# First tile's centring, transposes and evacuation in halves, x ahead of the weight rows on ScalarE's queue, TensorE warmed on constants, variances by ScalarE

## Chip, cores, metric

One core of one Trainium2 chip. The metric is the device time of one execution in microseconds (us); three executions of the kernel before gave a median of 1615.57 us (1615.40 to 1615.64). All times inside a profile are counted from the start of its span.

## The reference, cut to what matters

Two layers, each a sliding-window attention block and a gated feed-forward block on x of 2048 tokens by 1024 columns. What matters here is the very beginning: layer norm of the first tokens, then their projection on the first 1024 columns of `wqkv`.

```python
def _layernorm(x, axis=-1, eps=1e-5):
    m = jnp.mean(x, axis=axis, keepdims=True)
    v = jnp.var(x, axis=axis, keepdims=True)
    return (x - m) / jnp.sqrt(v + eps)
...
    x = A_x                                              # (1, 2048, 1024), bf16
    x = x + _A_ref(_layernorm(x, axis=-1), A_wqkv, A_wo) # qkv = x @ wqkv; attention; @ wo
    x = x + _B_ref(_layernorm(x, axis=-1), B_w1, B_w3, B_w2)
    ...                                                  # the same two blocks once more
```

## The kernel before: the parts that count

The kernel records every operation in a small program (`pr.add`). A scheduler in Python (`place`) then gives each a modelled start time, from durations and a model of the transfers, and the operations are emitted in the order of those times. So the order on each engine follows from modelled times, and an edit can move operations that it does not touch.

The first stage works on four tiles of 128 tokens. Tiles 0 and 1 are only centred; their scale is applied later. They are transposed by TensorE, copied out of PSUM and projected against the eight weight rows (a "row" is 128 of the 1024 input columns, 256 KB) as these arrive. Tiles 2 and 3 are fully normalized, transposed and projected in a second half, which needs all eight rows.

```python
def q_first():
    for hh in range(2):                                  # x tile 0 in two halves, one on each queue
        dma(128, x_sb[0][:, hh * 512:(hh + 1) * 512], ..., queue="AQ" if hh else "SP")
    load_x(0, 1, 2)                                      # x tile 1, SyncE's queue
    rows = q_weights(0, "k", load=False)
    for kk in range(3):
        rows[2](kk, "SP" if kk == 1 else "AQ")           # rows 0 and 2 on ScalarE's queue
    load_x(0, 2, 4)                                      # x tiles 2 and 3
    for kk in range(3, KT):
        rows[2](kk)                                      # rows 3 to 7
    ...
    for j in range(2):
        dve(0.5, lambda _, j=j: nc.vector.tensor_scalar(xn[j][:], x_sb[j][:], mean[:, j:j + 1], None,
                                                        op0=ALU.subtract), ...)
        transposed(xn[j], ...)                           # 8 transposes, then two copies out of one bank
    for j in range(2, TPC):
        stats(j); root(j, j + 1); apply(j); transposed(xn[j], ...)
    for j in range(2):
        stats(j, [("xn", TPC - 1)]); root(j, j + 1); apply(j); dma(..., transpose=True)
    ...
    # projection of tiles 0 and 1: rows 0, 1, 2 by tile (8 matmuls each), rows 3 to 7 for both (8 wide ones each)
    for kk, j0, j1 in [(k, j, j + 1) for j in range(2) for k in range(3)] + [(k, 0, 2) for k in range(3, KT)]:
        ...
```

"AQ" is ScalarE's queue, "SP" SyncE's. Transfers share eight semaphores in turn, so a transfer's issue may first wait for the landing of the one that had its semaphore before.

Of the kernel before, what the change touches and what calls it, by code (L numbers as in the profile page):

```python
# [33 lines left out]
class Program:  # L34
# [28 lines left out]
    def place(self, n_banks=8, rate=330e3):  # L63
# [18 lines left out]
        banks = [0.0] * n_banks  # L82
        pipe = 0.0
        left = len(self.ops)
# [9 lines left out]
        while left:  # L94
# [28 lines left out]
            if e in ("SP", "AQ"):  # L123
                free[e] = t + op.dur
                begin = max(pipe, t + 1.3)
                pipe = begin + op.size / rate
                op.end = pipe + 0.8
            else:
                free[e] = t + op.dur
                op.end = t + op.dur + op.lag  # L130
# [24 lines left out]
def kernel(  # L155
# [42 lines left out]
    def alloc(name, shape, dt=BF16):  # L198
        return sb.tile(shape, dt, name=name)
# [4 lines left out]
    preload = alloc("preload", [P, 1], FP32)  # L204
    warm = alloc("warm", [P, CH])
    x_sb = [alloc(f"x{n}", [P, D]) for n in range(S // P)]
# [40 lines left out]
    def dve(dur, emit, reads, writes, cls=2, **kw):  # L247
        return pr.add("DVE", dur, emit, reads, writes, cls, **kw)
# [29 lines left out]
    pr.add("POOL", 0.1, lambda _: nc.gpsimd.memset(epst[:], EPS), writes=["eps"])  # L278
    dve(0.3, lambda _: nc.vector.memset(warm[:], 0.0), [], ["warm"], 0)
    act(1.5, lambda _: nc.scalar.activation(preload[:], epst[:], ACTF.Sqrt), ["eps"], ["preload"])  # L280
    for i in range(NWARM):
        a = Acc()
        pr.add("PE", 0.43, lambda op: nc.tensor.matmul(bank[op.takes[0].bank][:], lhsT=warm[:, 0:P], rhs=warm[:],
                                                       start=True, stop=True), reads=["warm"], takes=[a])

# [16 lines left out]
    def ln(c, first=False):  # L302
        s = stage_no[0]
        b, q = s % 2, s % 4
        xb = xnT[b]

        def stats(j, after=()):
            n = c * TPC + j
            pri = -9 if first else 1
            for hh in range(2):  # L310
                dve(0.67, lambda _, hh=hh: nc.vector.bn_stats(st[q][:, j, hh, :],  # L311
                                                              x_sb[n][:, hh * 512:(hh + 1) * 512]),
                    [("x", n, hh)] + list(after), [("st", q, j, hh)], pri)
            dve(0.2, lambda _: nc.vector.bn_aggr(mv[q][:, j, :], st[q][:, j, :, :]),  # L314
                [("st", q, j, 0), ("st", q, j, 1)], [("mv", q, j)], pri)

        def root(j0, j1):
            act(0.3, lambda _: nc.scalar.activation(sd[q][:, j0:j1], mv[q][:, j0:j1, 1], ACTF.Sqrt, bias=epst[:]),  # L318
                [("mv", q, j) for j in range(j0, j1)] + ["eps"], [("sd", q, j) for j in range(j0, j1)], -9 if first else 0, table="sqrt")
            dve(0.16, lambda _: nc.vector.reciprocal(rstd[q][:, j0:j1], sd[q][:, j0:j1]),  # L320
                [("sd", q, j) for j in range(j0, j1)], [("rstd", q, j) for j in range(j0, j1)], -9 if first else 0)

        def apply(j):
            n = c * TPC + j
            dve(0.5, lambda _: nc.vector.tensor_scalar(xn[j][:], x_sb[n][:], mv[q][:, j, 0:1], rstd[q][:, j:j + 1],  # L325
                                                       op0=ALU.subtract, op1=ALU.mult),
                [("x", n, 0), ("x", n, 1), ("mv", q, j), ("rstd", q, j)], [("xn", j)], -9 if first else 1)

        if first:
            return b, q, stats, root, apply  # L330
        for j in range(TPC):
            stats(j)
        root(0, TPC)
        for j in range(TPC):
            apply(j)
            dma(256, xb[:, :, j * P:(j + 1) * P], xn[j][:], [("xn", j)], [("xnT", b, j)], 0, transpose=True)
        return b
# [17 lines left out]
    def q_weights(which, split, load=True, after=()):  # L355
        ids = [take_slot(), take_slot()]
        if not load:
            def row(kk, queue="SP"):
                i = ids[kk // 4]
                v = slot[i][:].rearrange("p (k c) -> p k c", k=4)  # L360
                dma(256, v[:, kk % 4, :], wqkv_v[:, kk, which * D:(which + 1) * D], [], [("w", i, kk % 4)], 0,
                    queue=queue)
            return ids, split, row
# [28 lines left out]
    def q_tile(l, c, which, ws, b, keep=None):  # L392
        for m0 in range(0, KT, 2):
            i = n_sgt[0] % 4
            n_sgt[0] += 1
            for m in (m0, m0 + 1):
                a = Acc()
                lk = [q_lhs(ws, kk, m) for kk in range(KT)]
                op = mm8(a, [(w, xnT[b][:, kk, :]) for kk, (w, _) in enumerate(lk)], True, True,
                         list({k for _, k in lk}) + [("xnT", b, j) for j in range(TPC)])  # L400
                evac(act, 0.59, lambda _, a=a, i=i, m=m: nc.scalar.copy(sgt[i][:, m % 2, :], bank[a.bank][:]), op, [],  # L401
# [13 lines left out]

    def transposed(src, key, dst, dkeys, both):
        a = Acc()

        def tr(op):
            pt = bank[a.bank][:].bitcast(BF16)  # L420
            for kk in range(KT):
                nc.tensor.transpose(pt[:, kk * P:(kk + 1) * P], src[:, kk * P:(kk + 1) * P], ident[:])  # L422
        tro = pr.add("PE", 0.5, tr, [key, "ident"], [], takes=[a], lag=0.17, lane=2)

        def ev(add, fn, k0, k1, dur):
            def emit(op):
                pt = bank[a.bank][:].bitcast(BF16)
                fn(dst[:, k0:k1, :], pt.rearrange("p (k t) -> p k t", k=KT)[:, k0:k1, :])
            evac(add, dur, emit, tro, [], dkeys[k0:k1], a, cls=-9)
        if both:  # L430
            ev(dve, nc.vector.tensor_copy, 0, 4, 0.68)
            ev(act, nc.scalar.copy, 4, 8, 0.59)
        else:
            ev(act, nc.scalar.copy, 0, 8, 1.0)

    def q_first():
        for hh in range(2):
            dma(128, x_sb[0][:, hh * 512:(hh + 1) * 512], xin[:, 0, hh * 512:(hh + 1) * 512], [], [("x", 0, hh)], 0,
                queue="AQ" if hh else "SP")
        load_x(0, 1, 2)  # L440
        rows = q_weights(0, "k", load=False)
        wslots[0] = rows[:2]
        for kk in range(3):
            rows[2](kk, "SP" if kk == 1 else "AQ")
        load_x(0, 2, 4)
        for kk in range(3, KT):
            rows[2](kk)
        b, q, stats, root, apply = ln(0, first=True)
# [4 lines left out]
        act(0.75, lambda _: nc.scalar.activation(xn[3][:, 0:512], x_sb[0][:, 512:1024], ACTF.Copy,  # L453
                                                 accum_out=part[:, 1:2]), [("x", 0, 1)], [("xn", 3), ("part", 1)], -9)
        dve(0.16, lambda _: nc.vector.tensor_scalar(mean[:, 0:1], part[:, 0:1], part[:, 1:2], 1.0 / D, op0=ALU.add,
                                                    op1=ALU.mult), [("part", 0), ("part", 1)], [("mean", 0)], -9)
# [3 lines left out]
        for j in range(2):  # L460
            dve(0.5, lambda _, j=j: nc.vector.tensor_scalar(xn[j][:], x_sb[j][:], mean[:, j:j + 1], None,  # L461
                                                            op0=ALU.subtract),
                [("x", j, 0), ("x", j, 1), ("mean", j)], [("xn", j)], -9)
            transposed(xn[j], ("xn", j), ce[:, :, j * P:(j + 1) * P], [("ce", j, k) for k in range(KT)], True)
        for j in range(2, TPC):
            stats(j)
            root(j, j + 1)
            apply(j)
            transposed(xn[j], ("xn", j), xnT[b][:, :, j * P:(j + 1) * P], [("xnT", b, j)] * KT, False)
        for j in range(2):  # L470
            stats(j, [("xn", TPC - 1)])
            root(j, j + 1)
            apply(j)
            dma(256, xnT[b][:, :, j * P:(j + 1) * P], xn[j][:], [("xn", j)], [("xnT", b, j)], 0, transpose=True)
# [27 lines left out]
        for g in range(4):  # L502
            lk = [[q_lhs(wslots[0], kk, m)[0] for kk in range(KT)] for m in (2 * g, 2 * g + 1)]

            def emit(op, g=g, lk=lk, pa=pa):
                for m in range(2):
                    for kk in range(KT):
# [3 lines left out]
            ops.append(pr.add("PE", 16 * 0.1092, emit,  # L511
                              [("w", i, k) for i in wslots[0][0] for k in range(4)] + [("xnT", b, 2), ("xnT", b, 3)],
                              [], takes=[pa[g]], lag=0.17))
# [10 lines left out]
        for which, key, tile_ in ((1, "kT", kT), (2, "vT", vT)):  # L524
            dve(0.11, lambda _, tile_=tile_: nc.vector.memset(tile_[:, :, 0:HALO], 0.0), [], [(key, "h")], 1)
            q_tile(0, 0, which, wslots[which], b, (key, tile_))
        for t0, t1_ in ((0, 2), (2, 4), (4, 6), (6, 7), (7, 8)):
            dma(256 * (t1_ - t0), wo[:, t0:t1_, :], wo_v[:, t0:t1_, :], [("d", 0, 2, 0, 6)], [("wo", t0)], 3)
# [26 lines left out]
    def t_stage(l, half):  # L555
# [54 lines left out]
        for j in range(TCH // P):  # L610
            n = tok0 // P + j
            for hh in range(2):
                a = Acc()
                op = mm8(a, [(oT[oh][:, t, j * P:(j + 1) * P], wo[:, t, hh * 512:(hh + 1) * 512]) for t in range(KT)],
                         True, True, [("oT", oh, t) for t in range(KT)] + [("wo", t) for t in (0, 2, 4, 6, 7)], lane=1)
                xs = x_sb[n][:, hh * 512:(hh + 1) * 512]
# [5 lines left out]
    def b_stage(l, c):  # L622
        b = ln(c)
        allx = [("xnT", b, j) for j in range(TPC)]
        for g0 in range(0, NF, 4):
# [119 lines left out]
```

## Time and profile before

| | before |
|---|---|
| median of 3, us | 1615.57 |
| TensorE busy | 100% |
| TensorE's last pause ends | 6.89 us |
| first projection matmul | 7.34 us |
| first of the 64 second-half matmuls | 15.28 us |
| first K matmul (first 512-wide one on data) | 22.27 us |
| first K matmul's start to last matmul's start | 1588.615 us |

The last three numbers come from the trace's list of matmul starts. They make a precise instrument: the body from the first K matmul to the last matmul never pauses, so its time is fixed, and whatever the first stage gains or loses is read off the start of the first K matmul.

Next, from the page of the kernel before, are the shares of the chain of waits: first by engine, then by line. In all lines of the profile PE is TensorE, PEld its weight loads, DVE VectorE, ACT ScalarE, SP SyncE; a q behind it (ACTq) marks what the engine's sequencer does itself, such as issuing a transfer.

```profile
PE 99%; DMA 0%; ACT 0%; DVE 0%; SPq 0%; issue 0%; ACTq 0%
PE bank L344 98%; PE bank L494 0%; PE bank L508 0%; DMA x<-in_A_x_dram 0%; PE bank L422 0%; ACT xn L457 0%; DVE xn L461 0%; SPq L260 0%; DVE x L672 0%; ACTq L457 0%
```

TensorE is the whole chain. Only its start can move. The timeline of TensorE in the kernel before, from 3 to 16 us, has the start in us, the time covered, engine, line, operation, tiles, shape, count, and in brackets the idle time before it and what ended it:

```profile
5.25 0.62 PE L422 MATMUL bank<-ident,xn 128*128 128x128 bf16 x8 [0.28 <-DVE xn L461]
6.89 0.62 PE L422 MATMUL bank<-ident,xn 128*128 128x128 bf16 x8 [1.02 <-DVE xn L461]
7.34 5.46 PE L494 MATMUL bank<-hT,slot 128*128 128x128 bf16 x72
12.64 1.06 PE L422 MATMUL bank<-ident,xn 128*128 128x128 bf16 x16
13.54 1.91 PE L494 MATMUL bank<-hT,slot 128*128 128x256 bf16 x16
15.28 0.93 PE L508 MATMUL bank<-xnT,slot 128*128 128x256 bf16 x7
```

L422 are the transposes, L494 the projection of tiles 0 and 1, L508 that of tiles 2 and 3. The pause of 1.02 us is a wait for tile 1's centring. Tile 0 has been transposed since 5.87 us but stands behind tile 1 everywhere: its projection in TensorE's order, and the first half of its copy out of PSUM in VectorE's, after tile 1's centring (ScalarE began the second half at 6.22, after tile 1's sum):

```profile
6.34 0.49 DVE L461 TENSOR_SCALAR xn<-x,mean 128x1024 bf16<-128x1024 bf16 x1 [1.15 <-ACT xn L457]
6.81 0.42 DVE L428 COPY hT<-bank 128x512 bf16<-128x512 bf16 x1
```

(Matmuls overlap, so idle time as the view has it is some 0.16 us less than the distance between starts in excess of full pace.)

### The profile page before, as it was taken

The numbers are of one execution on the slowest core, as the hardware profiler recorded it, in microseconds if no ns is written. First come the engines' busy times: TensorE is split into PE (matmuls) and PEld (weight loads), VectorE is DVE, ScalarE is ACT, GpSimd is POOL, SyncE is SP. The second block draws the span as 40 slices with busy tenths as digits, with TensorE's granted clock in tenths as the row PEclk, the third lists the DMA queues.
The fourth block names the chain that finished last, engine by engine and source line by source line (L and its number), as shares of the span: only waits on it lengthen the run. The fifth ranks groups of instructions, "written<-read, shape, count | busy, mean of one in ns | idle before, by whom it ended". The sixth has DMA issues, their size and how long they took to land.

```text
span 1613.7 us, 19216 instructions
## 1 busy us (share of the span) xinstructions
PE 1608.6 (100%) x7610; PEld 762.6 (47%) x7610; DVE 1123.6 (70%) x1908; ACT 326.8 (20%) x521; POOL 4.9 (0%) x28
## 2 busy tenths in 40 slices
PE   9999999999999999999999999999999999999999
PEld 6555544444444444444444444444444444444444
DVE  5898888989888888988888829884288832211211
ACT  4423322021201222113211032110321101101110
POOL 1000000000000000000000000000000000000000
PEclk9999999999999999999999999999999999999999
DMA  9834755485548764858554487355873564454441
GB/s 313 234 103 151 221 170 171 131 211 170 171 137 250 195 190 133 216 167 243 181 161 134 160 243 231 123 171 176 251 225 118 157 183 156 144 174 152 156 164 45
DMA packets 350651, 285.80 MB, mean 177 GB/s; under 512 B 72290, under 2 KB 344930, under 8 KB 350562
## 3 DMA queue, kind: packets, MB, share of 16 engines
q1 hardware_dynamic: 350128, 283.94, 58.6%
q8 instruction: 59, 0.97, 0.3%
q10 hardware_dynamic: 432, 0.66, 0.1%
q14 instruction: 32, 0.25, 0.1%
HBM read 238.94 MB, written 29.36 MB: 166 GB/s over the span
## 4 chain that ended last, share of the span: by engine, by line
PE 99%; DMA 0%; ACT 0%; DVE 0%; SPq 0%; issue 0%; ACTq 0%
PE bank L344 98%; PE bank L494 0%; PE bank L508 0%; DMA x<-in_A_x_dram 0%; PE bank L422 0%; ACT xn L457 0%; DVE xn L461 0%; SPq L260 0%; DVE x L672 0%; ACTq L457 0%
## 5 line engine op out<-in xcount | busy, mean ns | idle before, releaser
L344 PE MATMUL bank<-xnT,slot 128*128 128x512 bf16 x5056 | 1094.2, 379 | 0.0
L344 PEld LDWEIGHTS <-slot 128*128 128x128 bf16 x5056 | 518.1, 102 | 573.0
L344 PE MATMUL bank<-slot,hT 128*128 128x512 bf16 (+2 forms) x1848 | 389.2, 373 | 0.0
L642 DVE TENSOR_TENSOR hT<-sg,bank 128x512 bf16<-128x512 bf16 x224 | 153.4, 685 | 215.7 <-PE bank L344 203.4
L264 DVE TENSOR_TENSOR scr<-scr 128x1024 bf16<-128x1024 bf16 (+3 forms) x576 | 292.9, 539 | 2.0
L344 PEld LDWEIGHTS <-hT 128*128 128x128 bf16 x1848 | 178.6, 98 | 208.7
L640 ACT ACTIVATE sg<-bank 128x512 bf16<-128x512 f32 x224 | 133.7, 597 | 662.6 <-PE bank L344 625.3
L264 DVE TENSOR_TENSOR scr<-qT,kT 128x2048 bf16<-128x2048 bf16 x128 | 154.1, 1220 | 72.1 <-DMA kT<-qkv_d 70.7
L401 ACT CAST sgt<-bank 128x512 bf16<-128x512 f32 x184 | 107.5, 586 | 349.7 <-PE bank L344 345.5
L264 DVE TENSOR_TENSOR scr<-pA,vT 128x2048 bf16<-128x2048 bf16 x128 | 152.3, 1220 | 0.3
L672 DVE TENSOR_TENSOR x<-x,bank 128x512 bf16<-128x512 bf16 (+1 forms) x66 | 43.9, 670 | 123.4 <-PE bank L344 123.4
L344 PE MATMUL bank<-wo,oT 128*128 128x512 bf16 x512 | 113.1, 379 | 0.0
L311 DVE BATCH_NORM_STATS2 st<-x 128x6 f32<-128x512 bf16 x128 | 84.3, 680 | 10.6 <-DMA x<-in_A_x_dram 10.2
L344 PEld LDWEIGHTS <-oT 128*128 128x128 bf16 x512 | 50.1, 98 | 60.3
L617 DVE TENSOR_TENSOR x<-x,bank 128x512 bf16<-128x512 bf16 x64 | 43.9, 685 | 31.5 <-PE bank L344 30.6
L600 DVE STREAM_TRANSPOSE pA<-pB 128x2048 bf16<-128x2048 bf16 x16 | 37.0, 2311 | 0.5
L577 DVE STREAM_TRANSPOSE pB<-pA 128x2048 bf16<-128x2048 bf16 x16 | 37.0, 2310 | 0.4
L264 DVE TENSOR_TENSOR pA<-scr 128x256 bf16<-128x256 bf16 x128 | 35.8, 286 | 0.4
L318 ACT ACTIVATE sd<-mv,epst 128x4 f32<-128x4 f32 (+1 forms) x19 | 5.7, 299 | 143.8 <-DVE mv L314 143.7
L325 DVE TENSOR_SCALAR xn<-x,mv,rstd 128x1024 bf16<-128x1024 bf16 x64 | 32.0, 541 | 3.5 <-DMA xnT<-xn 3.3
L640 ACT ACT_TABLE_LOAD x19 | 24.4, 1283 | 49.4 <-PE bank L344 49.2
L264 DVE TENSOR_TENSOR oT<-scr 128x256 bf16<-128x256 bf16 x128 | 33.9, 288 | 0.1
(55 smaller groups left out, 203.8 us busy)
## 6 DMA issues: line engine op xcount, KB each, us to landing
slot<-in_B_w_dram SPq DMA_DIRECT2D x160, 1024.0 KB, 5.9
slot<-in_A_wqkv_dram SPq DMA_DIRECT2D x28, 1024.0 KB, 5.2
qkv_d<-sgt SPq DMA_DIRECT2D x92, 256.0 KB, 3.5
qT<-qkv_d SPq DMA_DIRECT2D x16, 512.0 KB, 4.8
slot<-in_B_w_dram SPq DMA_DIRECT2D x16, 512.0 KB, 5.8
kT<-qkv_d SPq DMA_DIRECT2D x14, 544.0 KB, 5.9
vT<-qkv_d SPq DMA_DIRECT2D x14, 544.0 KB, 5.9
out_dram<-x SPq DMA_DIRECT2D x31, 128.0 KB, 4.4
```

Of the source, the lines that this page charges most:

```text
L264: return lambda _: nc.vector.tensor_tensor(o, a, b, op=op)
L311: dve(0.67, lambda _, hh=hh: nc.vector.bn_stats(st[q][:, j, hh, :], x_sb[n][:, hh * 512:(hh + 1) * 512]), [("x", n, hh)] + list(after), [( ...
L318: act(0.3, lambda _: nc.scalar.activation(sd[q][:, j0:j1], mv[q][:, j0:j1, 1], ACTF.Sqrt, bias=epst[:]), [("mv", q, j) for j in range(j0, ...
L325: dve(0.5, lambda _: nc.vector.tensor_scalar(xn[j][:], x_sb[n][:], mv[q][:, j, 0:1], rstd[q][:, j:j + 1], op0=ALU.subtract, op1=ALU.mult), ...
L344: nc.tensor.matmul(bank[a.bank][:, 0:ncol], lhsT=w, rhs=r, start=first and i == 0, stop=last and i == n - 1)
L401: evac(act, 0.59, lambda _, a=a, i=i, m=m: nc.scalar.copy(sgt[i][:, m % 2, :], bank[a.bank][:]), op, [], [("sgt", i, m % 2)], a)
L577: dve(2.31, lambda _: nc.vector.transpose(psmT[:].rearrange("p c d -> p (c d)"), psm[:].rearrange("p w s -> p (w s)")), allA, ["pB"])
L600: dve(2.31, lambda _: nc.vector.transpose(At[:].rearrange("p w s -> p (w s)"), AeT[:].rearrange("p c d -> p (c d)")), ["pB"], allA)
L617: evac(dve, t1(512), lambda _, xs=xs, a=a: nc.vector.tensor_tensor(xs, xs, bank[a.bank][:], op=ALU.add), op, [("x", n, hh)], [("x", n, hh) ...
L640: evac(act, 0.6, lambda _, i=i, a=ag: nc.scalar.activation(sg[i][:], bank[a.bank][:], ACTF.Silu), og, [], [("sg", i)], ag, table="silu")
L642: evac(dve, t1(512), lambda _, i=i, a=au, f=f: nc.vector.tensor_tensor(hT[:, f, :], sg[i][:], bank[a.bank][:], op=ALU.mult), ou, [("sg", i ...
L672: evac(dve, t1(cn), lambda _, xs=xs, a=a, cn=cn: nc.vector.tensor_tensor(xs, xs, bank[a.bank][:, 0:cn], op=ALU.add), op, [("x", n, hh)], [ ...
```

## The change

Its intent: let tile 0's projection start before tile 1 is ready (halves), get x tile 1 sooner (ScalarE's queue, nothing but x ahead of it), relieve VectorE of two tiles' statistics, and start the warm-up without waiting for a fill. The core of the diff, cut (dependency keys, the scheduler's model of two queues and the split of a later load left out):

```diff
-    dve(0.3, lambda _: nc.vector.memset(warm[:], 0.0), [], ["warm"], 0)
-    act(1.5, lambda _: nc.scalar.activation(preload[:], epst[:], ACTF.Sqrt), ["eps"], ["preload"])
+    one = nc.const_aps.tensor(1.0, [P, CH], BF16)
+    act(1.5, lambda _: nc.scalar.activation(preload[:], nc.const_aps.tensor(0.0, [P, 1], FP32), ACTF.Sqrt), [],
+        ["preload"])
...
-        load_x(0, 1, 2)
+        dma(256, x_sb[1][:], xin[:, 1, :], [], [("x", 1, 0), ("x", 1, 1)], 0, queue="AQ")
...
-        for kk in range(3):
-            rows[2](kk, "SP" if kk == 1 else "AQ")
+        for kk in range(4):
+            rows[2](kk)
         load_x(0, 2, 4)
-        for kk in range(3, KT):
-            rows[2](kk)
+        rows[2](4)
+        rows[2](5)
...
+        rows[2](6, 2, queue="AQ", after=[("part", 1)])       # rows 6 and 7 as one transfer
...
-            dve(0.5, lambda _, j=j: nc.vector.tensor_scalar(xn[j][:], x_sb[j][:], mean[:, j:j + 1], None,
+            for h0, h1 in ((0, 1), (1, 2)) if j == 0 else ((0, 2),):
+                dve(0.5 if j else 0.32, lambda _, j=j, c0=512 * h0, c1=512 * h1: nc.vector.tensor_scalar(
+                    xn[j][:, c0:c1], x_sb[j][:, c0:c1], mean[:, j:j + 1], None, op0=ALU.subtract),
...                                                            # transposes: two banks, 4 each, one copy each
-            stats(j, [("xn", TPC - 1)])
-            root(j, j + 1)
-            apply(j)
+            act(1.25, lambda _, j=j: nc.scalar.activation(..., x_sb[j][:], ACTF.Square, bias=mean[:, j:j + 1],
+                                                          scale=-1.0, accum_out=part[:, j:j + 1]), ...)
+            act(0.3, ...Sqrt...); dve(0.16, ...reciprocal...); dve(0.5, ...normalize...)
```

More of the change, by code (lines that the diff above doesn't have):

```diff
@@ L82, in place @@
         banks = [0.0] * n_banks
-        pipe = 0.0
+        pipe = {"SP": 0.0, "AQ": 0.0}
         left = len(self.ops)
@@ L124, in place @@
                 free[e] = t + op.dur
-                begin = max(pipe, t + 1.3)
-                pipe = begin + op.size / rate
-                op.end = pipe + 0.8
+                begin = max(pipe[e], t + 1.3)
+                other = pipe["AQ" if e == "SP" else "SP"]
+                both = min(op.size / (0.6 * rate), max(0.0, other - begin))
+                pipe[e] = begin + both + (op.size - both * 0.6 * rate) / rate
+                op.end = pipe[e] + 0.8
             else:
@@ L204 @@
     preload = alloc("preload", [P, 1], FP32)
-    warm = alloc("warm", [P, CH])
     x_sb = [alloc(f"x{n}", [P, D]) for n in range(S // P)]
@@ L278 @@
     pr.add("POOL", 0.1, lambda _: nc.gpsimd.memset(epst[:], EPS), writes=["eps"])
-    dve(0.3, lambda _: nc.vector.memset(warm[:], 0.0), [], ["warm"], 0)
-    act(1.5, lambda _: nc.scalar.activation(preload[:], epst[:], ACTF.Sqrt), ["eps"], ["preload"])
+    one = nc.const_aps.tensor(1.0, [P, CH], BF16)
+    act(1.5, lambda _: nc.scalar.activation(preload[:], nc.const_aps.tensor(0.0, [P, 1], FP32), ACTF.Sqrt), [],
+        ["preload"])
     for i in range(NWARM):
         a = Acc()
-        pr.add("PE", 0.43, lambda op: nc.tensor.matmul(bank[op.takes[0].bank][:], lhsT=warm[:, 0:P], rhs=warm[:],
-                                                       start=True, stop=True), reads=["warm"], takes=[a])
+        pr.add("PE", 0.43, lambda op: nc.tensor.matmul(bank[op.takes[0].bank][:], lhsT=one[:, 0:P], rhs=one,
+                                                       start=True, stop=True), takes=[a])
     n_sgt = [0]
@@ L326, in apply @@
                                                        op0=ALU.subtract, op1=ALU.mult),
-                [("x", n, 0), ("x", n, 1), ("mv", q, j), ("rstd", q, j)], [("xn", j)], -9 if first else 1)
+                [("x", n, 0), ("x", n, 1), ("mv", q, j), ("rstd", q, j)], [("xn", j)] + [("xn", j, h) for h in range(2)], -9 if first else 1)
         if first:
@@ L335, in ln @@
             apply(j)
-            dma(256, xb[:, :, j * P:(j + 1) * P], xn[j][:], [("xn", j)], [("xnT", b, j)], 0, transpose=True)
+            dma(256, xb[:, :, j * P:(j + 1) * P], xn[j][:], [("xn", j)],
+                [("xnT", b, j)] + [("xnT", b, j, h) for h in range(2)], 0, transpose=True)
         return b
@@ L357, in q_weights, with row @@
         if not load:
-            def row(kk, queue="SP"):
+            def row(kk, n=1, after=(), **kw):
                 i = ids[kk // 4]
                 v = slot[i][:].rearrange("p (k c) -> p k c", k=4)
-                dma(256, v[:, kk % 4, :], wqkv_v[:, kk, which * D:(which + 1) * D], [], [("w", i, kk % 4)], 0,
-                    queue=queue)
+                dma(256 * n, v[:, kk % 4:kk % 4 + n, :], wqkv_v[:, kk:kk + n, which * D:(which + 1) * D], after,
+                    [("w", i, kk % 4 + z) for z in range(n)], 0, **kw)
             return ids, split, row
@@ L399, in q_tile @@
                 op = mm8(a, [(w, xnT[b][:, kk, :]) for kk, (w, _) in enumerate(lk)], True, True,
-                         list({k for _, k in lk}) + [("xnT", b, j) for j in range(TPC)])
+                         list({k for _, k in lk}) + [("xnT", b, j) for j in range(TPC)] +
+                         [("xnT", b, j, h) for j in range(TPC) for h in range(2)])
                 evac(act, 0.59, lambda _, a=a, i=i, m=m: nc.scalar.copy(sgt[i][:, m % 2, :], bank[a.bank][:]), op, [],
@@ L414, in q_stage, with transposed, tr, emit @@
         stage_no[0] += 1
-    def transposed(src, key, dst, dkeys, both):
-        a = Acc()
-        def tr(op):
-            pt = bank[a.bank][:].bitcast(BF16)
-            for kk in range(KT):
-                nc.tensor.transpose(pt[:, kk * P:(kk + 1) * P], src[:, kk * P:(kk + 1) * P], ident[:])
-        tro = pr.add("PE", 0.5, tr, [key, "ident"], [], takes=[a], lag=0.17, lane=2)
-        def ev(add, fn, k0, k1, dur):
-            def emit(op):
-                pt = bank[a.bank][:].bitcast(BF16)
-                fn(dst[:, k0:k1, :], pt.rearrange("p (k t) -> p k t", k=KT)[:, k0:k1, :])
-            evac(add, dur, emit, tro, [], dkeys[k0:k1], a, cls=-9)
-        if both:
-            ev(dve, nc.vector.tensor_copy, 0, 4, 0.68)
-            ev(act, nc.scalar.copy, 4, 8, 0.59)
-        else:
-            ev(act, nc.scalar.copy, 0, 8, 1.0)
+    def transposed(src, keys, dst, dkeys):
+        for h, add, fn, dur in ((0, dve, nc.vector.tensor_copy, 0.42), (1, act, nc.scalar.copy, 0.59)):
+            a = Acc()
+            k0 = 4 * h
+            def tr(op, a=a, k0=k0):
+                pt = bank[a.bank][:].bitcast(BF16)
+                for k in range(4):
+                    nc.tensor.transpose(pt[:, k * P:(k + 1) * P], src[:, (k0 + k) * P:(k0 + k + 1) * P], ident[:])
+            tro = pr.add("PE", 0.25, tr, [keys[h], "ident"], [], takes=[a], lag=0.17, lane=2)
+            def emit(op, a=a, k0=k0, fn=fn):
+                pt = bank[a.bank][:].bitcast(BF16)
+                fn(dst[:, k0:k0 + 4, :], pt[:, 0:4 * P].rearrange("p (k t) -> p k t", k=4))
+            evac(add, dur, emit, tro, [], dkeys[k0:k0 + 4], a, cls=-9)
     def q_first():
@@ L460, in q_first @@
         for j in range(2):
-            dve(0.5, lambda _, j=j: nc.vector.tensor_scalar(xn[j][:], x_sb[j][:], mean[:, j:j + 1], None,
-                                                            op0=ALU.subtract),
-                [("x", j, 0), ("x", j, 1), ("mean", j)], [("xn", j)], -9)
-            transposed(xn[j], ("xn", j), ce[:, :, j * P:(j + 1) * P], [("ce", j, k) for k in range(KT)], True)
+            for h0, h1 in ((0, 1), (1, 2)) if j == 0 else ((0, 2),):
+                dve(0.5 if j else 0.32, lambda _, j=j, c0=512 * h0, c1=512 * h1: nc.vector.tensor_scalar(
+                    xn[j][:, c0:c1], x_sb[j][:, c0:c1], mean[:, j:j + 1], None, op0=ALU.subtract),
+                    [("x", j, 0), ("x", j, 1), ("mean", j)], [("xn", j)] + [("xn", j, h) for h in range(h0, h1)], -9)
+            transposed(xn[j], [("xn", j, h) for h in range(2)], ce[:, :, j * P:(j + 1) * P],
+                       [("ce", j, k) for k in range(KT)])
         for j in range(2, TPC):
@@ L468, in q_first @@
             apply(j)
-            transposed(xn[j], ("xn", j), xnT[b][:, :, j * P:(j + 1) * P], [("xnT", b, j)] * KT, False)
+            transposed(xn[j], [("xn", j)] * 2, xnT[b][:, :, j * P:(j + 1) * P],
+                       [("xnT", b, j, k // 4) for k in range(KT)])
         for j in range(2):
-            stats(j, [("xn", TPC - 1)])
-            root(j, j + 1)
-            apply(j)
+            act(1.25, lambda _, j=j: nc.scalar.activation(sgt[j][:].rearrange("p a b -> p (a b)"), x_sb[j][:],
+                                                          ACTF.Square, bias=mean[:, j:j + 1], scale=-1.0,
+                                                          accum_out=part[:, j:j + 1]),
+                [("x", j, 0), ("x", j, 1), ("mean", j)] + [("ce", 1, KT - 1)],
+                [("part", j), ("sgt", j, 0), ("sgt", j, 1)], -8)
+            act(0.3, lambda _, j=j: nc.scalar.activation(sd[q][:, j:j + 1], part[:, j:j + 1], ACTF.Sqrt, bias=epst[:],
+                                                         scale=1.0 / D),
+                [("part", j), "eps"], [("sd", q, j)], -8, table="sqrt")
+            dve(0.16, lambda _, j=j: nc.vector.reciprocal(rstd[q][:, j:j + 1], sd[q][:, j:j + 1]), [("sd", q, j)],
+                [("rstd", q, j)], 0)
+            dve(0.5, lambda _, j=j: nc.vector.tensor_scalar(xn[j][:], x_sb[j][:], mean[:, j:j + 1],
+                                                            rstd[q][:, j:j + 1], op0=ALU.subtract, op1=ALU.mult),
+                [("x", j, 0), ("x", j, 1), ("mean", j), ("rstd", q, j), ("xn", TPC - 1)],
+                [("xn", j)] + [("xn", j, h) for h in range(2)], 0)
             dma(256, xnT[b][:, :, j * P:(j + 1) * P], xn[j][:], [("xn", j)], [("xnT", b, j)], 0, transpose=True)
@@ L511, in q_first @@
             ops.append(pr.add("PE", 16 * 0.1092, emit,
-                              [("w", i, k) for i in wslots[0][0] for k in range(4)] + [("xnT", b, 2), ("xnT", b, 3)],
+                              [("w", i, k) for i in wslots[0][0] for k in range(4)] +
+                              [("xnT", b, j, h) for j in (2, 3) for h in range(2)],
                               [], takes=[pa[g]], lag=0.17))
@@ L526, in q_first @@
             q_tile(0, 0, which, wslots[which], b, (key, tile_))
-        for t0, t1_ in ((0, 2), (2, 4), (4, 6), (6, 7), (7, 8)):
+        for t0, t1_ in ((0, 2), (2, 4), (4, 5), (5, 6), (6, 7), (7, 8)):
             dma(256 * (t1_ - t0), wo[:, t0:t1_, :], wo_v[:, t0:t1_, :], [("d", 0, 2, 0, 6)], [("wo", t0)], 3)
@@ L614, in t_stage @@
                 op = mm8(a, [(oT[oh][:, t, j * P:(j + 1) * P], wo[:, t, hh * 512:(hh + 1) * 512]) for t in range(KT)],
-                         True, True, [("oT", oh, t) for t in range(KT)] + [("wo", t) for t in (0, 2, 4, 6, 7)], lane=1)
+                         True, True, [("oT", oh, t) for t in range(KT)] + [("wo", t) for t in (0, 2, 4, 5, 6, 7)], lane=1)
                 xs = x_sb[n][:, hh * 512:(hh + 1) * 512]
@@ L623, in b_stage @@
         b = ln(c)
-        allx = [("xnT", b, j) for j in range(TPC)]
+        allx = [("xnT", b, j) for j in range(TPC)] + [("xnT", b, j, h) for j in range(TPC) for h in range(2)]
         for g0 in range(0, NF, 4):
```

## The prediction

> **What bounds the kernel.** TensorE. The page gives PE 100% busy; the chain of waits is 99% PE. Setting each matmul's start against the next one's, the only stretches below full pace are the warm matmuls and two pauses before the projection: 0.28 us, and one between 5.65 and 6.89 us. From 6.89 us (transposes of tile 1) to 1611 us the stream never pauses; the waits view agrees (PE waits 1.3 us in all for the centred tiles). So the change can only move the start of the unbroken stream, and must not open a hole in it.
>
> **The chain before (timeline).** x tile 0 lands 3.43/3.62; mean by 4.67; centring 4.71 to 5.19; 8 transposes 5.25 to 5.87. Then PE waits for tile 1: landed 5.07, ScalarE sum 5.16 to 6.31, centring 6.34 to 6.83, transposes 6.89, projection from 7.34. The projection of tile 0 stands in PE's order behind tile 1's transposes.
>
> **What changes.**
> 1. PE order now: transposes of tile 0, 16 matmuls of tile 0 (weight rows 0 and 1), transposes of tile 1, 32 small matmuls, 32 of the 40 wide ones, 16 transposes, 8 wide. Tile 0's work fills the pause.
> 2. Centring in halves (0.48 us for the whole; estimate 0.35 for a half): transposes start near 5.1, VectorE's 0.42 us copy of the first half ends near 6.0. First projection matmul near 6.0 instead of 7.34; as 0.45 us of transposes now come later, the stream starts 6.89 - 6.02 = 0.87 us earlier. The second half's copy waits on ScalarE behind tile 1's sum, but only rows 4 to 7 need it.
> 3. x tile 1 moves to ScalarE's queue. There row 0 landed at 4.89 against 5.07 for x on the other: about 0.2 us. ScalarE's program now has the table load (1.28 us) ahead of its DMA issues. The Trainium skill (Perfetto Trace Analysis, Per-instruction lifecycle) has the sequencer push an ACT instruction and go on; the trace agrees, a sequencer event at 177.87 lies inside a table load of 176.79 to 178.08. So I expect issues near 0.8 us, not 2.1.
> 4. Warm matmuls start near 0.75 instead of 1.19: no gain by itself.
> 5. Variances of tiles 0 and 1 by ScalarE take 4 x 0.64 us off VectorE; off PE's path.
>
> **What is given back.** At the trace's 0.66 us per 256 KB, with rows 6 and 7 (512 KB) sharing the rings from about 5 us and rows 0 to 3 ahead of x tiles 2 and 3, those land near 8.8 and 9.5 instead of 7.16 and 7.84. Their statistics (0.64 us each), root and normalizing end near 13.1, transposes near 13.6, the four evacuations near 14.6, about when PE, 0.87 us ahead, needs them (14.5). Row 4 arrives near 10.1 against a need at 10.0. I take 0.2 us off.
>
> **Prediction.** Net gain about 0.65 us: 1614.9 us; 8 in 10 between 1614.2 and 1615.7. Faster by over 2%: 0.005; within 2%: 0.99; slower by over 2%: 0.005.
>
> **What would show it.** First projection matmul near 6.0; start of the 64 matmuls after the second transposes (15.28 before) near 14.65; first 512-wide K matmul (22.27) near 21.6; no pause after. Tile 0's second half should land near 3.4; after 4.2, the table load held the issue up. Tile 1 near 4.9. Tiles 2 and 3 near 9, VectorE idle before their statistics.
>
> **What would make it wrong.** DMA issues held behind the table load (gain near 0); rows 2 or 4, or tiles 2 and 3, later than estimated, opening holes; a clock granted later, slowing the transposes; a gain of 0.9 or more if tiles 2 and 3 are in time; a new stall far downstream, where the scheduler has shuffled VectorE and queue orders.

## The result, and the profile after

In the six executions of the changed kernel the median was 1616.01 us (1615.67 to 1616.29); the kernel before, in six, had 1615.61 (1615.40 to 1615.83). A ratio here is the mean time of one kernel's runs over that of the other's of the same rounds, so not quite the ratio of the medians quoted. It is 1.0003, with a 95% interval of 0.999 to 1.0016: the same by the 2% rule, and by the times alone not even sure to be slower. The traces say more.

The timeline of TensorE in the changed kernel, from 4 to 17 us:

```profile
4.98 0.66 PE L428 MATMUL bank<-ident,xn 128*128 128x128 bf16 x8
5.89 1.05 PE L509 MATMUL bank<-hT,slot 128*128 128x128 bf16 x16 [0.25 <-DVE hT L433]
6.96 0.62 PE L428 MATMUL bank<-ident,xn 128*128 128x128 bf16 x8
7.42 2.83 PE L509 MATMUL bank<-hT,slot 128*128 128x128 bf16 x40
11.16 2.79 PE L509 MATMUL bank<-hT,slot 128*128 128x256 bf16 x24 [0.91 <-DMA slot<-in_A_wqkv_dram]
13.79 1.06 PE L428 MATMUL bank<-ident,xn 128*128 128x128 bf16 x16
14.68 1.04 PE L509 MATMUL bank<-hT,slot 128*128 128x256 bf16 x8
15.56 1.69 PE L523 MATMUL bank<-xnT,slot 128*128 128x256 bf16 x14
```

The projection (L509) does start at 5.89 instead of 7.34. But after 40 matmuls TensorE stops for a weight transfer. The waits view of the changed kernel for TensorE (who waited for whom: total us, times, longest) puts it first:

```profile
PE bank L509 <- DMA slot<-in_A_wqkv_dram: 0.9, 1, 0.9
```

And in the page's chain of the changed kernel, by line, the transfer is a new member with 1% of the span:

```profile
PE bank L347 98%; DMA slot<-in_A_wqkv_dram 1%; PE bank L523 0%; PE bank L509 0%; PE bank L428 0%; SPq L261 0%; DVE x L688 0%
```

The account from the matmul starts: the unbroken stream would begin at 5.89 and not 6.89, a gain of 1.00 us; it loses 0.19 us before tile 1's transposes and 1.08 us before row 4's matmuls. The sum is 0.27 us lost, and the second half indeed starts at 15.56 against 15.28, the first K matmul at 22.54 against 22.27. From there to the last matmul both kernels take 1588.615 us, so the shuffled orders further on cost nothing here. The page of the changed kernel shows 7463 matmuls where 7610 were before; these are missing records (one about every 10.8 us, each a hole of exactly one matmul), not missing work.

Who is late? The landing times below are those of each transfer's last semaphore update in the trace, in us. "Position" is the sum of KB issued up to and with the transfer, both queues together.

| before | position | landed | | changed | position | landed |
|---|---|---|---|---|---|---|
| x tile 0 (two halves) | 256 | 3.43, 3.62 | | x tile 0 (two halves) | 256 | 3.28, 3.54 |
| row 0, x tile 1 | 768 | 4.89, 5.07 | | row 0, x tile 1 | 768 | 4.96, 5.15 |
| rows 2, 1 | 1280 | 6.21, 6.41 | | rows 1, 2 | 1280 | 5.70, 6.53 |
| x tiles 2, 3 | 1792 | 7.16, 7.84 | | row 3, x tile 2 | 1792 | 7.71, 8.65 |
| row 3 | 2048 | 8.50 | | rows 6 and 7 | 2304 | 9.74 |
| row 4 | 2304 | 9.17 | | x tile 3 | 2560 | 10.44 |
| rows 5, 6 | 2816 | 9.86, 10.52 | | **row 4** | **2816** | **11.11** |

TensorE wants row 4 at 10.09 (eight wide matmuls after 9.21). It landed at 11.11, because 512 KB that are wanted later, rows 6 and 7, were issued at 3.57 us and stand ahead of it. That row 4 itself was issued late, at 5.71, is not the cause: in a second profile of this kernel (e5) it was issued at 6.30 and landed at 11.13, 0.02 us later.

### The profile page after: what moved, and what is told of

Its sections match the earlier page's. It is cut to its first block, busy times and chain, and to the rows that moved or that the text cites. A ratio compares the mean times of both kernels' runs of the same rounds, so it can differ in the third digit from the quotient of the medians.

```text
span 1614.2 us, 19079 instructions
## 1 busy us (share of the span) xinstructions
PE 1601.5 (99%) x7463; PEld 762.6 (47%) x7610; DVE 1121.5 (69%) x1904; ACT 331.3 (21%) x527; POOL 5.2 (0%) x28
## 4 chain that ended last, share of the span: by engine, by line
PE 99%; DMA 1%; issue 0%; SPq 0%; DVE 0%
PE bank L347 98%; DMA slot<-in_A_wqkv_dram 1%; PE bank L523 0%; PE bank L509 0%; PE bank L428 0%; SPq L261 0%; DVE x L688 0%
```

## The experiments

Theory A: the order of the rows costs what the halves gain. Rivals: two queues lose bandwidth (B), the halves gain nothing (C), one odd execution. Each experiment names its own (no run has the number e6). Summary (each median is of that kernel's runs, with the kernel before of the same rounds beside it; "tile 1" is the landing of x tile 1; pauses are in excess of full pace, from the matmul starts after 6.5 us):

| run | time | before | tile 1 | first projection | first K | pauses |
|---|---|---|---|---|---|---|
| before | 1615.57 | | 5.07 | 7.34 | 22.27 | none |
| changed | 1616.01 | 1615.61 | 5.15 | 5.89 | 22.54 | 0.19, 1.08 |
| e1, rows 6, 7 last | 1614.99 | 1615.74 | 5.58 | 6.60 | 21.98 | none |
| e2, rows 4, 5 first | 1615.07 | 1615.74 | 5.00 | 6.14 | 21.51 | none |
| e3, halves alone | 1616.76 | 1615.74 | 5.34 | 7.61 | 22.54 | 1.01 at 188 us |
| e4, issues alone | 1618.44 | 1615.74 | 5.37 | 9.50 | 25.36 | (2.53 from 6.09) |
| e5, changed again | 1615.92 | 1615.63 | 5.04 | 5.86 | 22.56 | 0.06 at 6.7, 1.20 |
| e7, variances on VectorE | 1616.49 | 1615.63 | 6.09 | 5.92 | 22.40 | 1.09, 0.93 at 188 us |
| e8, warm-up as before | 1618.45 | 1615.63 | 5.17 | 9.44 | 25.52 | (2.38 from 6.18) |
| e9, halves with order forced | 1617.19 | 1615.63 | 4.72 | 6.57 | 22.92 | 0.25, 0.25, 0.46, 1.07 at 188 us |
| e10, before again (1 run) | 1615.45 | 1615.37 | 4.98 | 7.25 | 22.18 | none |
| e11, e1 again | 1614.89 | 1615.37 | 4.98 | 6.14 | 21.52 | none |
| e12, e7 again (1 run) | 1616.51 | 1615.37 | 5.25 | 5.93 | 22.22 | 0.24, 0.59, 0.97 at 188 us |
| e13, e9 again (1 run) | 1617.04 | 1615.37 | 4.98 | 6.58 | 22.71 | 0.14, 0.46, 1.07 at 188 us |

All gave correct results. All timed runs with several executions were in the fast state; of the three kernels with one run the state is unknown, so only their profiles are used. By the 2% rule each of those with several executions is "same".

### e1: rows 6 and 7 last, on SyncE's queue

```diff
-        rows[2](4)
-        rows[2](5)
+        for kk in range(4, KT):
+            rows[2](kk)
...
-        rows[2](6, 2, queue="AQ", after=[("part", 1)])
```

> The changed kernel with one thing taken back: weight rows 6 and 7 are issued one by one on SyncE's queue behind row 5, not as one transfer on ScalarE's queue ahead of x tile 3 and rows 4 and 5. Theory A (order: the 512 KB of rows 6 and 7, which TensorE needs last, are served before x tile 3 and rows 4 and 5): row 4 lands near 9.3 us instead of 11.11, before it is needed at 10.09; the pause of 1.07 us behind the first 8 wide matmuls is gone; the 64 matmuls of the second half start near 14.48 (15.56 in the changed kernel, 15.28 before), the first K matmul near 21.47 (22.54, 22.27 before), the time near 1614.8 us. Theory B (the rows come late because two queues at work, or the many single rows, lose bandwidth): row 4 lands after 10.1, part of the pause stays, first K matmul after 21.9. Theory C (the halves and the new order of TensorE's work gain nothing by themselves): the pause goes elsewhere, first K matmul near 22.3.

Row 4 landed at 9.88 and the pause was gone, so A holds against C, and the time fell to 1614.99 (ratio to before 0.9996). In this execution x tile 0 landed only at 4.00 and 4.25, so everything starts 0.7 us later than in the changed kernel's profile and the first K matmul is at 21.98 and not at 21.47. B is not excluded by this run, as row 4 is later than 9.3.

### e2: the same bytes on the same queues, other rows

```diff
-        rows[2](4)
-        rows[2](5)
+        rows[2](6)
+        rows[2](7)
...
-        rows[2](6, 2, queue="AQ", after=[("part", 1)])
+        rows[2](4, 2, queue="AQ", after=[("part", 1)])
```

> The changed kernel, but the one transfer on ScalarE's queue carries weight rows 4 and 5, and rows 6 and 7 follow on SyncE's queue behind x tile 3. The queues carry the same bytes at the same times as in the changed kernel; only which rows they are differs. Theory A (order): rows 4 and 5 land together near 9.75 us, before the need at 10.09, no pause there; x tile 3 still lands near 10.44, so its normalized tile is ready near 13.3 and the second transposes and evacuations cost 0.2 to 0.4 us; the 64 matmuls start near 14.75, the first K matmul near 21.75, the time near 1615.1. Theory B (two queues lose time): the transfer on ScalarE's queue still lands too late, pause over 0.5 us, first K matmul at 22.2 or later.

This is the sharpest test: only which rows travel when is changed. Rows 4 and 5 landed at 9.93, TensorE came to row 4 at 10.14. The timeline of TensorE in e2:

```profile
6.14 1.05 PE L509 MATMUL bank<-hT,slot 128*128 128x128 bf16 x16
7.03 0.61 PE L428 MATMUL bank<-ident,xn 128*128 128x128 bf16 x8
7.47 5.45 PE L509 MATMUL bank<-hT,slot 128*128 128x128 bf16 x64
12.76 1.06 PE L428 MATMUL bank<-ident,xn 128*128 128x128 bf16 x16
13.65 1.04 PE L509 MATMUL bank<-hT,slot 128*128 128x256 bf16 x8
14.52 1.69 PE L523 MATMUL bank<-xnT,slot 128*128 128x256 bf16 x14
```

No bracket is left: the 64 matmuls from 7.47 run through where the changed kernel stopped after 40. The first K matmul is at 21.51, 1.03 us ahead of the changed kernel and 0.76 ahead of the kernel before; the time is 1615.07 (ratio 0.9996), all four runs (1614.98 to 1615.14) under all seven of the kernel before (1615.21 to 1616.26). B falls as the cause of the pause: the second queue carried the same load. The expected 0.2 to 0.4 us for tile 3 did not come: the second transposes and copies were in time.

### e3: halves alone on the kernel before

```diff
-            dve(0.5, ... xn[j][:], x_sb[j][:], mean[:, j:j + 1] ...)          # and the rest of the halves' edit
+            for h0, h1 in ((0, 1), (1, 2)) if j == 0 else ((0, 2),):
+                dve(0.5 if j else 0.32, ...)
```

> The kernel before with only the centring, transposes and evacuation in halves (issue order of the transfers, variances and warm-up as before). The scheduler leaves TensorE's order as before here: both tiles' transposes, then the projection. Theory A says the halves are worth nothing without tile 0's matmuls standing ahead of tile 1's transposes: tile 0's transposes start near 5.05 instead of 5.25, tile 1's still at 6.89, first K matmul 22.27 give or take 0.05, time 1615.6. Theory C' (halves as such shorten the chain): first K matmul 0.3 us or more earlier.

The first K matmul is 0.27 us later than before, and tile 1 landed 0.27 us later (5.34 against 5.07), so the halves by themselves moved nothing: with TensorE's order unchanged, tile 1 decides. The time, 1616.76, was not expected. The trace has a pause of 1.01 us at 188 us, where the last of four DMA transposes comes late; the edit had moved the scheduler's modelled times and thereby an order far downstream.

### e4: the new issues alone

```diff
-        load_x(0, 1, 2)
+        dma(256, x_sb[1][:], xin[:, 1, :], ..., queue="AQ")
...                                                                # rows 0 to 3, tiles 2 and 3, rows 4 and 5
+        rows[2](6, 2, queue="AQ", after=[("part", 1)])
```

> The kernel before with only the new issues: x tile 1 on ScalarE's queue, rows 0 to 3 ahead of x tiles 2 and 3, rows 6 and 7 on ScalarE's queue (warm-up, halves and variances as before). Theory A: rows 4 and tile 3 land as late as in the changed kernel (11.1 and 10.4 us); TensorE, which comes to row 4 near 10.96 here, pauses some 0.2 us for it and some 0.2 us more for tile 3's transposes or evacuations; first K matmul near 22.65, time 1615.9 to 1616.1, slower than before. Theory B' (the issues are harmless, something else in the change cost the time): first K matmul at 22.27 or earlier.

A miss, and no clean test. Here is ScalarE's timeline in e4:

```profile
4.67 0.19 ACT L455 ACTIVATION_READ_ACCUMULATOR xn<-x 128x1 f32 x1
6.45 0.39 ACTq L258 DMA_DIRECT2D slot<-in_A_wqkv_dram  x1
6.95 1.06 ACT L460 ACTIVATE xn<-x 128x1024 bf16<-128x1024 bf16 x1 [2.09 <-DMA slot<-in_A_wqkv_dram]
```

Tile 1 landed at 5.37, but its sum started at 6.95: the issue of rows 6 and 7 stood ahead of it in ScalarE's program and waited for the semaphore of row 1, which landed at 6.43. In the changed kernel the same issue got tile 0's semaphore and went at 3.57. Then the clock fell. These are two stretches of e4: the stretch and its length, busy time (count) of PE, PEld, DVE, ACT and POOL, granted clock, DMA share, GB/s.

```profile
4.61:8.02 3.41, 1.21 (x11) 0.54 (x9) 0.73 (x4) 1.33 (x5) 0.00 (x0) 1.00 0.95 335
8.02:11.43 3.41, 2.76 (x27) 2.76 (x28) 2.58 (x6) 1.14 (x3) 0.00 (x0) 0.50 1.04 396
```

After a stretch in which TensorE was busy for 1.21 of 3.41 us, the clock was halved for the next 3.41 us. What the new issues alone cost without this hold-up stays open.

### e5: the changed kernel again

```diff
(no edit)
```

> The changed kernel once more, to see whether its pause is there in a second profile and to get more times. Theory A (order of the rows): again a pause of 0.8 to 1.2 us behind the first 8 wide matmuls, ended by the landing of weight row 4 after 10.9 us; median 0.2 to 0.6 us over the kernel before. If the pause was a chance of one execution: none here, first K matmul near 21.6, median below the kernel before.

The pause is there again, 1.20 us, ended by row 4 at 11.13; the first K matmul is at 22.56. TensorE's timeline in e5 has it:

```profile
7.31 2.83 PE L509 MATMUL bank<-hT,slot 128*128 128x128 bf16 x40
11.18 2.79 PE L509 MATMUL bank<-hT,slot 128*128 128x256 bf16 x24 [1.04 <-DMA slot<-in_A_wqkv_dram]
```

### e7 and e12: variances back on VectorE (on e2)

```diff
-            act(1.25, ... ACTF.Square ... accum_out=part[:, j:j + 1] ...); act(0.3, ... ACTF.Sqrt ...)
-            dve(0.16, ... reciprocal ...); dve(0.5, ... tensor_scalar ...)
+            stats(j, [("xn", TPC - 1)])
+            root(j, j + 1)
+            apply(j)
```

> The kernel with rows 4 and 5 on ScalarE's queue (first K matmul 21.51), with the variances of tiles 0 and 1 back on VectorE by its statistics instructions, as before the change. If the move to ScalarE is off TensorE's path, as the prediction said: first K matmul within 0.1 us of 21.5. The rival, from the order of VectorE's instructions here (two statistics of tile 0 stand between the two copies of the second transposes): the copies end 0.7 us or more later and the 64 matmuls of the second half wait for them; first K matmul 22.0 to 22.4.

In e7 x tile 1 landed at 6.09, which put a pause of 1.09 us before its transposes and hid what was asked. So it ran again.

> The kernel with the variances back on VectorE, again, because x tile 1 landed a whole microsecond late in its first profile and hid what was asked. If tile 1 lands near 5.0 to 5.2: the prediction's reading (variances off TensorE's path) says no pause between 6.8 and 15 us and first K matmul near 21.5; the rival (VectorE's copies of the second transposes wait behind two statistics instructions) says a pause of 0.4 us or more before the 64 matmuls or before the last transposes, first K matmul after 21.9. The pause of 0.9 us at 188 us should be there again in both.

TensorE's timeline in e12:

```profile
7.52 4.58 PE L498 MATMUL bank<-hT,slot 128*128 128x128 bf16 x56
12.52 0.62 PE L428 MATMUL bank<-ident,xn 128*128 128x128 bf16 x8 [0.42 <-DVE xn L327]
12.98 1.04 PE L498 MATMUL bank<-hT,slot 128*128 128x256 bf16 x8
```

The first K matmul is 0.71 us later than in e2, 0.59 of it by this pause. The cause is neither of the two expected: VectorE's copies were in time (no pause before the last 64), but the scheduler now placed tile 2's transposes after 56 matmuls instead of 64, at 11.94, when tile 2 was ready only at 12.46. The pause near 188 us came too. So the move to ScalarE is worth something in this kernel, through the orders it leads to. That VectorE's 2.6 us of statistics as such matter was not shown.

### e8: warm-up as before (on e2)

```diff
-    one = nc.const_aps.tensor(1.0, [P, CH], BF16)
-    act(1.5, lambda _: nc.scalar.activation(preload[:], nc.const_aps.tensor(0.0, [P, 1], FP32), ACTF.Sqrt), [],
+    dve(0.3, lambda _: nc.vector.memset(warm[:], 0.0), [], ["warm"], 0)
+    act(1.5, lambda _: nc.scalar.activation(preload[:], epst[:], ACTF.Sqrt), ["eps"], ["preload"])
```

> The kernel with rows 4 and 5 on ScalarE's queue (first K matmul 21.51), with the warm-up as before the change (VectorE fills a tile, the first activation waits for the epsilon tile). As a cost on the engines this is at most 0.4 us of warm-up that nothing waits for, so by the prediction: no change. But the built order differs: the scheduler now leaves TensorE's 16 transposes together, issues ScalarE's two x transfers before the table load, and the transfer of rows 4 and 5, placed ahead of tile 1's sum, waits for the landing of row 1. So the rival: tile 1's sum starts after 6 us, the transposes of tile 1 after 7.7, first K matmul 23.0 or later and the time 1616.5 or more.

The first K matmul is at 25.52 and the time 1618.45. The rival holds, and by more than expected: as in e4 the issue on ScalarE's queue waited for row 1 (landed 6.37), tile 1's sum began at 6.88, TensorE paused 2.38 us, and the clock was at half from 8.17 to 11.58. The edit costs no engine anything worth speaking of. In the scheduler's model it delays the warm-up and one activation. Building e2 with one of the two put back at a time (nothing was run) tells them apart: the filled tile alone puts TensorE's 16 transposes together again, so that tile 0 no longer goes first; the activation alone gives the issue on ScalarE's queue the semaphore of row 1. e8 has both; what each of them costs was not measured.

### e9 and e13: halves on the kernel before, order forced

```diff
+            if j == 0:
+                copied = made[0][1]          # tile 0's copy
+            else:
+                cen.deps.add(copied)         # ahead of tile 1's centring
...
+            if (kk, j0, j1) == (1, 0, 1):
+                made[0][0].deps.add(op)      # tile 1's transposes behind tile 0's rows 0 and 1
```

> The kernel before with the halves alone, but two dependencies added to the scheduler's program so that tile 0's matmuls of rows 0 to 2 stand ahead of tile 1's transposes and tile 0's copy ahead of tile 1's centring; transfers, variances and warm-up as before. If the gain is in this order of TensorE's work and the new issues add nothing: the first projection matmul near 6.0 us, the second-half matmuls near 14.6, first K matmul 21.5 to 21.7 when x tile 0 lands by 3.6 us (later by as much as it lands later). If the new issues were needed for it: a pause for row 2, row 3 or row 4, and first K matmul after 22.0. The halves-alone kernel had a pause of 1.0 us at 188 us, from the order in which later transfers stand; it may recur here and would then hide the gain in the time.

> The kernel before with halves and the forced order, again. Its first profile had pauses of 0.25, 0.25 and 0.46 us, as weight rows 1 and 2 landed at 7.2 and 7.9 and x tile 2's statistics stood ahead of a copy. If those landings were a chance of that execution: rows 1 and 2 by 6.5, first K matmul at 21.5 to 21.9. If they belong to the order of issue (x tiles 2 and 3 share the rings with rows 1 and 2): again pauses for rows 1 and 2, first K matmul after 22.2. The pause of 1.0 us at 188 us recurs in both.

Both missed the good case, partly by my own design. The forced order put three rows of tile 0 ahead of tile 1's transposes and left nothing to do between these and the copy, which stood behind a statistics instruction: 0.46 us each time. Rows 1 and 2 landed at 7.22 and 7.93, then at 7.27 and 7.08, and cost 0.5 and 0.14 us. In e13 the full clock was granted only at 6.96 us, so the first 24 matmuls took 1.51 us beside the pause, instead of 1.34. So whether halves and order give the whole gain without the new issues stays open; with the old order of issue, rows 1 and 2 do tend to come too late for it.

### e10: the kernel before again

```diff
(no edit)
```

> The kernel before, profiled a second time, to see how far one execution's landings differ from another's. Expected: the body from the first K matmul to the last again 1588.615 us; first K matmul at 22.27 if x tile 1 lands near 5.1 us, later by as much as tile 1 lands later; no pause behind it. If weight rows 1 and 2 land after 7 us here too (6.4 and 6.2 in the first profile), the late rows of the halves kernels belong to the order of issue and not to the halves.

The first K matmul is at 22.18, the body again 1588.615 us. Rows 1 and 2 landed at 7.34 and 7.15, 0.9 us later than in the first profile, although issued within 0.01 us of the same times; the kernel before does not need them before 7.7, and there was no pause. So landings of equal programs differ by up to a microsecond between executions. By the expectation, the late rows 1 and 2 of e9 and e13 belong to the old order of issue and not to the halves: in four of the five profiles with that order (all but the first) both landed after 7 us.

### e11: e1 again, with more rounds

```diff
(the kernel of e1)
```

> The changed kernel with rows 6 and 7 last on SyncE's queue, again, with more rounds. Theory A (order of the rows): median 0.5 to 1.0 us below the kernel before of the same rounds and about 1 us below the changed kernel (1615.9 to 1616.0); no pause behind the first 8 wide matmuls; first K matmul between 21.4 (x tile 0 landed by 3.6) and 22.0 (landed at 4.2).

With x tile 0 landed at 3.34 and 3.52, row 4 came at 9.61, there was no pause, and the first K matmul is at 21.52, as in e2. The median of five is 1614.89 (1614.70 to 1615.17) against 1615.37 (1615.22 to 1615.80), ratio 0.9997, interval 0.9984 to 1.0011. e1 and e2 beat both kernels, by half to three quarters of a microsecond over the kernel before; as a share of 1615 us this is "same", and each 95% interval of the ratios includes 1. The runs of e2 and e11 all lie below those of the kernel before in the same rounds.

## Why the prediction was wrong

**The step that failed** is in "What is given back": "Row 4 arrives near 10.1 against a need at 10.0. I take 0.2 us off." The need was right (10.09). The arrival was 11.11, then 11.13, and the term that I sized at 0.2 us was 1.08 and 1.20 us. With it the sum turns from a gain into a loss. e2 shows it with one edit: other rows in the same transfer, 1.03 us back.

Why it was mis-sized: I reckoned with 0.66 us per 256 KB from too early a starting point (worked back, 10.1 less 8 times 0.66 puts the first 768 KB at 4.8 us; tile 1, the last of these, had landed at 5.07), and did not check the result against the one number in the profile before that answers it. Row 4 of the changed kernel stands at position 2816 KB; in the kernel before row 6 has this position, and it landed at 10.52. That alone would have made the pause some 0.4 us. The rest is the lag of single parts of a transfer. Each transfer updates its semaphore 16 times. Of row 4 in the changed kernel 15 updates had come by 10.59, and the last came at 11.11; in e5 14 had come by 10.62, the last two at 11.02 and 11.13; of row 6 in the kernel before all 16 had come by 10.52. Why a part lags was not tested.

Landings differ between executions, so more than one profile is needed. Over seven profiles (the kernel before and its repeat, the changed kernel and its repeat, e1, e11, e2) the row at 2816 KB landed between 10.5 and 11.3 us (10.52, 11.28, 11.11, 11.13, 11.19, 10.94, 10.86). In the five of them that had row 4 at 2304 KB it landed between 9.2 and 9.9 (9.17, 9.93, 9.88, 9.61, 9.93); e7 and e12, with e2's order of issue, had it there at 10.28 and 10.09. For a need at 10.1, the first place was late in every profile; the second was in time in these five, but with under 0.2 us to spare at the latest (9.93), and would not have been in e7.

Point by point:

- *TensorE bound, the body fixed*: right; 1588.615 us in both kernels.
- *Tile 0's work fills the pause, the projection starts near 6.0, 0.87 us gained*: right in kind and size. 5.89; 1.00 us less 0.19 for tile 1.
- *ScalarE's issues do not wait for the table load*: right. The changed kernel's ScalarE timeline:

```profile
0.73 1.28 ACT L281 ACT_TABLE_LOAD   x1 [0.73 <-PEq L745]
0.80 0.88 ACTq L257 DMA_DIRECT2D x<-in_A_x_dram  x2
```

  The two issues lie inside the load, as the Trainium skill (Perfetto Trace Analysis, Per-instruction lifecycle) has it of instructions that the sequencer pushes into a queue before it goes on to the next.
- *Tile 1 0.2 us sooner on ScalarE's queue*: wrong. It landed at 5.15 and 5.04 against 5.07 and 4.98. Its place (768 KB) had not changed.
- *Tiles 2 and 3 near 8.8 and 9.5*: 8.65 and 10.44. The second is another sign of the same error, but as TensorE paused for row 4, it was not what decided.
- *The warm-up no gain by itself, variances off TensorE's path*: true of the engines' time, wrong as a statement about the edits. e8 and e12 show that undoing either changes the built order and costs 4.0 and 0.7 us at the first K matmul.
- *No new stall far downstream*: right for this kernel. Three kernels that differ from it or from the kernel before by small edits (e3, e7, e9, and the last two again in their repeats) did get one of about 1 us at 188 us.

## What to carry to other kernels

When an early start is bought, list for each later operand its need and its place in the issue order, in bytes, and read the landing for that place off the profile at hand, with a margin (row 6 of the kernel before landed at 10.52 in one profile and at 11.28 in the other); an operand that is needed last and issued early delays all that come behind it, on whichever queue it travels. A transfer's issue in a compute engine's program is an instruction that can wait, and the work behind it waits too (in e4 and e8 tile 1's sum began 1.6 and 1.7 us after the tile had landed). Where a scheduler decides the order, compare built orders before believing that an edit is local.

## What the Trainium skill lacked or had wrong

- *DMA: Bandwidth & Descriptors, Queues, rings and completion order* has each DMA engine take turns between the queues it has work for. Here this did not show for two busy queues: the 512 KB issued on ScalarE's queue (q10) at 3.57 us moved almost nothing while older transfers of SyncE's queue (q1) were at work, and then nearly alone. The transfer view of the changed kernel by queue, in windows from 4.5 to 7 us and then from 7 to 8.5 us (packets, MB, share of the 16 engines' time):

```profile
q1 hardware_dynamic: 501, 0.93, 100.5%
q10 hardware_dynamic: 17, 0.01, 1.7%
...
q10 hardware_dynamic: 242, 0.48, 83.6%
q1 hardware_dynamic: 65, 0.10, 18.4%
```

  In e5 it was 478 packets against 19 in the first of these windows. This looks like service in order of issue across the queues. Why, and whether q10's work was at the DMA engines by then, was not tested.
- *The same page, Anatomy of one DMA*, fits setup and completion on GpSimd's path as a fixed cost per transfer. The page has no figure for how far the parts of one transfer drift apart: in e10 row 2's semaphore was updated first at 5.40 and last at 7.15 us, and in the first profile of the same program at 5.38 and 6.21; and a lag can stay, as in the changed kernel, where the last of 16 updates came over 0.5 us after the 15th for rows 6 and 7, x tile 3 and row 4 in turn (9.22 and 9.74, 9.93 and 10.44, 10.59 and 11.11).
- *TensorE: Matmul & The Clock Gate, What's actually happening* says that the clock falls after an idle window. In e4 it fell to half for 3.41 us after a window of the same length that was not idle: TensorE was busy for 1.21 us of it (1.17 in e8). In the kernel before, busy for 2.12 us from 4.17 to 7.58, it did not fall. That the window runs free of the kernel's start agrees: the full clock was granted between 3.98 us (e5) and 6.96 us (e13), and starting the warm-up 0.42 us earlier did not bring it sooner (4.33 in the changed kernel, 4.17 before).
